# The last store inside each exit block, and the last head pair's q and k loaded one iteration sooner, in an attention and mixture-of-experts kernel

## The chip, the cores and the metric

The kernel runs on one core of a Trainium2 chip. The metric is the device time of one execution in microseconds (us), over several runs; lower is better. One further execution is profiled, and all rows below are from that one. A head pair is two of the 48 (batch, head) combinations whose q and k are handled together; SP is the engine (SyncE) whose queue issues nearly all plain DMAs here.

## The reference

Causal attention over 4 batches of 12 heads, 448 positions, head size 64, and then a mixture of experts in which each of the 1792 tokens goes to the one expert of eight with the highest gate value:

```python
scores = scale * np.matmul(q, k.transpose(0, 1, 3, 2))
scores = np.where(mask, -1000000000.0, scores)
attn = softmax(scores)                       # in the reference's words: max, exp, sum, divide
x = np.matmul(attn, v) -> (1792, 768)
logits = x @ w_gate + modality_bias[modality_id]
e_idx = np.argmax(logits, axis=1)
for e in range(8):
    h = np.maximum(x[e_idx == e] @ w1[e], 0.0)          # 768 -> 1024
    out[e_idx == e] = gate_w[e_idx == e, None] * (h @ w2[e])   # 1024 -> 768
```

(The lines are shortened.) All is float32. The kernel gets float32 accuracy from TensorE by splitting operands into a high and a low part in the type fp32r and adding up several products.

## The kernel before, in words

The order of the work is written out by hand: the function `iteration(n)` (from line 1150) issues for n from 0 to 47 one step of a software pipeline, and each engine takes its instructions in the order in which they are issued. In iteration n the scores of head n are computed (`st_scores`, line 279: matmuls L297 on TensorE (PE), mask and row maximum L306 on VectorE (DVE)), the exponentials of head n-1 (ScalarE (ACT), L316), the transposes of head n-2 (PE, L328, split into high and low by ACT, L345, and DVE, L346), the product with v of head n-3 (PE, L359 and L366), and the output of head n-4, which PE combines at L420. Lists of further pieces (`later`, `before`, `soon`) are run at named iterations by `run_todo`: among them the stores of the attention's result x to DRAM (SP, L463), the loads of the first expert's weights w1 (SP, L719), the splits of these on GpSimd (POOL, L727 and L728), the gathers of x rows for the first blocks (POOL, L784), and the schedule of the experts' blocks (DVE and POOL, lines 560 to 640).

The q and k of pair m come in these steps. `load_qk(m)` loads both, 448 KB, on SP. `split_qk(m)`, on POOL, makes the high parts and q's low part (L196, L197); `stack_qk(m)`, on SP, copies them inside SBUF with four DMAs (L215 and L216) into a tile of its own, of which there are three in turn (m modulo 3), two of them in the pool and one elsewhere; `split_kl(m)` makes the rest on POOL. The last pair, m = 23 (`LATE`, line 239), goes another way: `late_load` (lines 241 to 250) loads plain q and k without a split straight into the tile of pair 20, with three DMAs (k at L244, the two halves of q at L248) and two memsets on POOL (L247), and its scores use two matmul operands instead of four. Pair 20's last reader is the scores of head 41; the first reader of pair 23's tile is the scores of head 46, and the first reader of pair 22's is the scores of head 44. In the kernel before, `late_load(23)` is issued in iteration 42, behind `st_scores(42)` and that iteration's `run_todo`, and `stack_qk(22)` at the head of iteration 41, ahead of `st_out`, the to-do list and the scores.

Behind the attention come the expert steps: eight fixed ones (t = 0 to 7), and then up to 16 small steps t = 8 to 23 (`tail(t)`, line 1474), each inside the If of the one before it (`tc.If(total > t)`), where `total` is a number that the schedule computed on the chip. Here total is 10, so that the small steps 8 and 9 run, and at t = 10 all engines branch out of the nest. A small step handles one half block of 64 rows. It ends with its second products on PE (`small_g2`, matmuls L878 and L882); their scaling with the gate value and the indirect store to the output are done by `half_y` (line 1394: ACT L924, DVE L925 for the two halves of a row, then POOL's indirect DMA, L1398) at the head of the next step, with the table `idg[(t - 1) % 3][0]` of row numbers and gate values. As the step that is last is only known on the chip, each small step copies its table into one fixed tile, `glast` (two DVE copies, L1463 to L1465), and behind the whole nest `half_y(glast)` (L1481) does it once more for the step that was last. `glast` is filled with an out-of-range row number at the start (POOL memset, L986).

At the If's exit the engines bring their semaphores to the values that the blocks not run would have left; in the profile these instructions have the line of the If, L1475. Behind the kernel's last line all engines drain their queues and meet; these instructions have L1522.

Of the kernel before, what the change touches and what calls it, by code (L numbers as in the profile page):

```python
# [11 lines left out]
I32 = mybir.dt.int32  # L12
# [9 lines left out]
def attention_moe(  # L22
# [58 lines left out]
    def cst(name, shape, dt=F32):  # L81
        return const.tile(shape, dt, name=name)
# [41 lines left out]
    tri0 = ctri = cst("ctri", [128, E, E])  # L124
    modi = cst("modi", [128, B * NTL, 2], I32)
    bias_sb = cst("bias_sb", [128, NM, 1, E])
    glast = cst("glast", [128, 2], I32)

    w1h, w1l = [], []
    raw1 = [early.tile([128, DF], F32, name=f"raw1{k}") for k in range(K1)]  # L130
# [110 lines left out]
    def late_load(m):  # L241
        b, j = divmod(m, H // 2)
        t = st_tile(m, F32)
        nc.sync.dma_start(out=t[:, 0, 1], in_=qk[b, j, :, 1])  # L244
        for a in range(2):
            r = slice(a * 64, a * 64 + 64)
            P.memset(t[64 - a * 64:128 - a * 64, a, 0], 0.0)  # L247
            nc.sync.dma_start(out=t[r, a, 0], in_=qk[b, j, r, 0])  # L248
            spl[2 * m + a] = (t[:, a, 0], t[:, 0, 1], None, None)

    vraws = [vraw, raw1[2].rearrange("p (t c) -> p t c", t=NTL)]

# [26 lines left out]
    def st_scores(g):  # L279
        qs, ks, qh, kl = spl.pop(g)  # L280
        banks = [bank("sa"), bank("sb")]
        nm = sm([128, NTL], "nm")
        p = praw[g % 3]

        outs, parts = {}, []
        for i, last in SORD:
            q0, n = QT[i]
            w = q0 + n
            bk, c0 = SPOS[i]
            if not last:  # L290
                outs[i] = banks[bk][:n, c0:c0 + w]
            if last and qh is None:
                continue
            a, z = (qh, kl) if last else (qs, ks)
            r = 128 if qh is None else n
            z0 = (128, 64, 64, 0)[i]
            nc.tensor.matmul(  # L297
                banks[bk][:r, c0:c0 + w], lhsT=a[:, q0:q0 + r], rhs=z[:, z0:z0 + w],
                start=(last == 0), stop=(last == 1 or qh is None),
            )  # L300
        for i in ORD:
            n = QT[i][1]
            w = QT[i][0] + n
            parts.append((i, n, outs[i], masks[i][:n], p[:n, POFF[i]:POFF[i] + w]))
        for i, n, o, m, z in parts:
            V.tensor_tensor_reduce(  # L306
                out=z, in0=o, in1=m, scale=-scale, scalar=3.0e38, op0=ALU.add, op1=ALU.min,
                accum_out=nm[:n, i:i + 1],
            )
        sc[g] = (p, parts, nm)  # L310
# [618 lines left out]
    with tc.manual_schedule():  # L929
# [53 lines left out]
        cthi = it[:, 64:64 + E * MAXB].rearrange("p (e b) -> p e b", b=MAXB)  # L983
        ctri_i = it[:, 192:192 + E * E].rearrange("p (e f) -> p e f", f=E)
        ti = it[:, 256:257]
        P.memset(glast, BIG)  # L986
        P.memset(onesf, 1.0 / STEP)
        P.memset(eq, 0.5)
        P.memset(sch_a, -float(STEP * SHIFT + 1))
# [29 lines left out]
        def run_todo(n):  # L1019
            for f in todo.pop(n, ()):  # L1020
                f()
# [127 lines left out]

        def iteration(n):  # L1150
            split = 7 < n + 3 < NHEAD and n + 3 >> 1 not in LATE
            if n % 2 == 1 and split:
                stack_qk((n + 3) // 2)
            gr, i = divmod(n - 2 * GH, GH)
            comb = 0 <= gr < B * NG
            if 0 <= n - 4 < NHEAD:
                st_out(n - 4)
            if comb:
                st_move(gr, i)
                st_norm(gr, i)  # L1160
                b, u = divmod(gr, NG)
                if u == NG - 1:
                    later(n + 1, lambda i=i: x_store(b, i))
                    if i == NTL - 1:
                        after_batch(b, n)
            run_todo((n,))
            if n in (2, 3):
                st_trans(n - 2)
            if n < NHEAD:
                st_scores(n)  # L1170
            run_todo(n)
            if n == 0:
                split_vh(0)
            if n % 2 == 1 and split:
                split_kl((n + 3) // 2)
            if n % 2 == 0 and 7 < n + 4 < NHEAD:
                (late_load if n + 4 >> 1 in LATE else split_qk)((n + 4) // 2)
            if n % GH == 1 and n > GH:
                st_sums(n // GH - 1)
            if n % GH == RECAT and n > GH:  # L1180
                st_rec(n // GH - 1)
            if 0 <= n - 1 < NHEAD:
                st_exp(n - 1)
            if 0 <= n - 2 < NHEAD:
                if n > 3:
                    st_trans(n - 2)
                run_todo(-n)
                st_split(n - 2)
            if 0 <= n - 3 < NHEAD:
                st_pv(n - 3)  # L1190
                st_low(n - 3)
            gr, i = divmod(n - 2 * GH + 1, GH)
            if 0 <= gr < B * NG:
                st_comb(gr, i)
            if n == 1:
                split_vl(0, V)
            if n == 2 or n % GH == 3 and n > GH and n // GH + 1 < B * NG:
                split_vh(n // GH + 1)
            if n == 2 or n % GH == 0 and n > GH:
                split_vl((n + 2) // GH, P)  # L1200
            if n == 4:
                V.memset(vraws[1][0:64, 3, :], 0.0)
            if n in (1, 3, 5, 7):
                load_qk(4 + n // 2)
            if n % 2 == 0 and n > 7 and n + 8 < NHEAD and n + 8 >> 1 not in LATE:
                load_qk((n + 8) // 2)
            if n in (1, 4):
                load_v(n // GH + 1)
            if n == 1:
                clear_tables()  # L1210
            if n % GH == 2 and n > GH and n // GH + 2 < B * NG:
                load_v(n // GH + 2)
# [190 lines left out]
        def step(t):  # L1403
            if t > SZ:
                half_y(idg[(t - 1) % 3][0])
            if SZ - 1 <= t and t + 1 < NSTEP:
                tc.mark_branch_hint_location(f"tail{t + 1}", reg(sch[t:t + 1, 5:6], HINTED, 0, 1), HINTED)
            ids_for(t + 2)
            nw = is_new(t)
            if t == 1:  # L1410
                with tc.If(nw < 1):
                    prefetch(0, raw1, w1, K1)
                    prefetch(0, raw2, w2, K2)

            wa, wb = (range(K2), None) if t < PZ else (range(K2 // 2), range(K2 // 2, K2))

            def w2_a():
                with tc.If(nw > 0):  # L1418
                    split_w(raw2, w2h, w2l, wa)
                    if wb is None:  # L1420
                        prefetch(t, raw2, w2, K2)

            def w2_b():
                with tc.If(nw > 0):
                    split_w(raw2, w2h, w2l, wb)
                    prefetch(t, raw2, w2, K2)

            def mid():
                if t + 1 == NSTEP:
                    return  # L1430
                next_x(t + 1, [x for _ in places_of(t + 1) for x in two_banks()])
                if t + 2 < NSTEP:
                    fetch_x(t + 2)
                with tc.If(is_new(t + 1) > 0):  # L1434
                    new_w1(t + 1)

            u = t % 2
            if t < PZ:
                w2_a()
                g1_pair()  # L1440
                part2(t, 0, of_pair(0), lambda: None, mid, [bank("ot"), bank("x")])
                ys = ht_banks()
                g2(ys, of_pair(1), range(K2))
                y_out(t, 1, ys)
                return
            if t < SZ:
                hb, pb = part1(u, w2_a, w2_b)
                part2(t, 0, of_block(u), lambda: h_trans(u, hb, 1, pb), mid, [bank("ot"), bank("x")])
                return
            oa, ob = two_banks()  # L1450
            pa, pb = ht_banks()
            w2_a()
            for k in range(4):
                for half, o in enumerate((oa, ob)):
                    small_g1(u, half, o, [k])
            for half, o in enumerate((oa, ob)):
                small_g1(u, half, o, range(4, K1))
                small_h(half, o)
            small_trans(u, 0, pa)
            small_trans(u, 1, pb)  # L1460
            w2_b()
            mid()
            g = idg[t % 3][0]  # L1463
            V.tensor_copy(glast[:, 0:1], g[:, 0:1])
            V.tensor_copy(glast[:, 1:2].bitcast(F32), g[:, 1:2].bitcast(F32))  # L1465
            small_g2(yl, u, range(2))
            for n in range(2):
                small_g2(yl, u, range(2, K2), [n])
# [3 lines left out]
        yl = [bank("ot"), bank("x")]  # L1472

        def tail(t):
            with tc.If(total > t, label=f"tail{t}"):  # L1475
                step(t)
                if t + 1 < NSTEP:
                    tail(t + 1)

        tail(SZ)  # L1480
        half_y(glast)  # L1481


_INS = ['qk', 'v', 'moe_modality_id', 'moe_w_gate', 'moe_modality_bias', 'moe_w1', 'moe_w2']
# [42 lines left out]
```

## Time and profile before

| | us |
|---|---|
| median of 3 runs | 489.51 |
| lowest and highest | 488.55, 492.07 |
| profiled execution, its own time | 491.61 |
| span of the profile | 489.9 |

| engine | busy us | share of the span | instructions |
|---|---|---|---|
| PE, matmul | 470.4 | 96% | 3219 |
| PE, weight load | 433.7 | 89% | 3219 |
| DVE | 291.6 | 60% | 864 |
| ACT | 277.9 | 57% | 696 |
| POOL | 237.1 | 48% | 320 |

The span runs from the first to the last instruction of the profiled execution; what the device time has beyond it lies around it. In the rows below a timeline's line gives start, duration, engine, line of the kernel, operation, output and input by their names in the program, shapes, and a count where equal neighbours are put together; what stands in brackets is the idle time of that engine just before, and what the profile takes to have ended it. A q behind an engine's name is its instruction queue: issues of DMAs, semaphores and branches. PEclk, the granted clock, is in parts of the full one. An attention iteration takes some 3.5 us in the stretch around 160 us.

### The profile page before, as it was taken

How to read it: one execution, taken by the hardware profiler on the slowest of the kernel's cores; microseconds unless marked ns; L12 is line 12 of the kernel's file. 1: busy time of each engine (PE TensorE's matmuls, PEld its weight loads, DVE VectorE, ACT ScalarE, POOL GpSimd, SP SyncE). 2: the span in 40 equal slices, each digit the busy share in tenths (PEclk: the TensorE clock that was granted, in tenths of full speed). 3: DMA queues.
4: the chain of work that ended last, by engine and by line, in shares of the span. 5: the costliest groups of instructions: out<-in, count | busy, mean ns of one | idle time of the engine just before them, and what ended most of it. 6: DMA issues, size and time to landing. Idle time of an engine off the chain costs nothing.

```text
span 489.9 us, 10098 instructions
## 1 busy us (share of the span) xinstructions
PE 470.4 (96%) x3219; PEld 433.7 (89%) x3219; DVE 291.6 (60%) x864; ACT 277.9 (57%) x696; POOL 237.1 (48%) x320
## 2 busy tenths in 40 slices
PE   8999999999999989989999999999999999999991
PEld 6789998998899868879999999999999999889770
DVE  7999999999999968787211126620130110283591
ACT  6899999999999967253312125620221111483670
POOL 7997999999999969952202004102001001021131
PEclk9999999999999989999999999999999999999997
DMA  7799789998996595523693006833001001086200
GB/s 191 221 261 250 210 218 282 247 228 237 242 238 148 135 314 189 185 91 97 194 411 111 33 1 226 304 118 101 33 0 55 33 14 52 33 285 204 96 15 4
DMA packets 43303, 77.25 MB, mean 158 GB/s; under 512 B 15582, under 2 KB 27614, under 8 KB 43232
## 3 DMA queue, kind: packets, MB, share of 16 engines
q1 hardware_dynamic: 40112, 65.30, 46.4%
q0 software_dynamic: 3040, 11.03, 6.6%
q8 instruction: 27, 0.44, 0.4%
q14 instruction: 44, 0.36, 0.2%
q10 hardware_dynamic: 80, 0.11, 0.1%
HBM read 48.10 MB, written 12.08 MB: 123 GB/s over the span
## 4 chain that ended last, share of the span: by engine, by line
PE 65%; DVE 14%; ACT 7%; issue 5%; POOL 4%; DMA 3%; POOLq 0%; DVEq 0%; ACTq 0%
PE g L803 7%; PE g L804 7%; PE g L805 7%; PE pt L328 4%; PE sa L297 4%; PE sb L297 4%; DVE p L306 3%; DVE pl L346 3%; ACT p L316 3%; PE ot L359 3%; PE ot L366 3%; PE x L420 2%; ACT ph L345 2%; PE ot L804 2%; DVE ut L390 2%
## 5 line engine op out<-in xcount | busy, mean ns | idle before, releaser
L784 POOL DMA_INDIRECT xg<-xs,idg x18 | 21.1, 1172 | 157.3 <-DVEq L1434 81.1
L316 ACT ACTIVATE p<-p,nm 128x448 f32<-128x448 f32 x192 | 94.7, 497 | 2.2 <-POOL eq L1039 1.9
L822 DVE SCALAR_TENSOR_TENSOR htl<-g,hth 128x256 fp32r<-128x256 f32 x40 | 16.7, 424 | 106.1 <-ACT hth L821 106.1
L803 PE MATMUL g<-xh,w1h 128*128 128x256 f32 x240 | 67.9, 283 | 0.3 <-DVE htl L822 0.3
L804 PE MATMUL g<-xl,w1h 128*128 128x256 f32 x240 | 67.8, 283 | 0.0
L805 PE MATMUL g<-xh,w1l 128*128 128x256 f32 x240 | 67.4, 281 | 0.0
L346 DVE TENSOR_TENSOR pl<-pt,ph 128x1024 fp32r<-128x1024 f32 x48 | 58.2, 1215 | 6.3 <-ACT ph L345 5.7
L345 ACT ACTIVATE ph<-pt 128x1024 fp32r<-128x1024 f32 x48 | 49.1, 1022 | 6.7 <-PE pt L328 5.9
L359 PE MATMUL ot<-ph,vhl 128*128 128x448 f32 x192 | 50.2, 302 | 2.0 <-DVE ut L390 1.0
L821 ACT ACTIVATE hth<-g 128x256 fp32r<-128x256 f32 x40 | 15.1, 382 | 65.0 <-PE g L805 62.0
L328 PE MATMUL pt<-ident,p 128*128 128x128 f32 x384 | 50.4, 275 | 0.0
L328 PEld LDWEIGHTS pt<-ident,p 128*128 128x128 f32 x384 | 45.5, 142 | 2.4 <-issue 0.7
L805 PEld LDWEIGHTS g<-xh,w1l 128*128 128x128 f32 x240 | 45.6, 190 | 0.0
L863 POOL DMA_INDIRECT out_dram<-row,idg x14 | 16.7, 1192 | 59.5 <-ACTq L1418 29.3
L803 PEld LDWEIGHTS g<-xh,w1h 128*128 128x128 f32 x240 | 45.0, 187 | 0.5 <-DVE htl L822 0.5
L804 PEld LDWEIGHTS g<-xl,w1h 128*128 128x128 f32 x240 | 45.0, 188 | 0.0
L306 DVE CUSTOM_DVE_ANT_0 p<-sa,mask 128x448 f32<-128x448 f32 x96 | 36.1, 412 | 3.4 <-PE sa L297 1.7
L359 PEld LDWEIGHTS ot<-ph,vhl 128*128 128x128 f32 x192 | 32.8, 189 | 5.8 <-DVE ut L390 1.8
L306 DVE CUSTOM_DVE_ANT_0 p<-sb,mask 128x192 f32<-128x192 f32 x96 | 36.3, 412 | 0.4 <-PE sb L297 0.4
L316 ACT ACTIVATION_READ_ACCUMULATOR p<-p,nm 128x1 f32 x192 | 36.4, 189 | 0.0
L366 PE MATMUL ot<-pl,vhl 128*64 128x64 f32 x192 | 34.5, 294 | 0.5 <-DVE pl L346 0.4
L390 DVE TENSOR_TENSOR ut<-ot,hol 64x448 f32<-64x448 f32 x48 | 29.4, 612 | 1.5 <-ACT hol L384 0.8
(389 smaller groups left out, 1298.2 us busy)
## 6 DMA issues: line engine op xcount, KB each, us to landing
raw<-in_moe_w_dram SPq DMA_DIRECT2D x24, 512.0 KB
st<-hl SPq DMA_DIRECT2D x52, 224.0 KB
raw<-in_qk_dram SPq DMA_DIRECT2D x19, 448.0 KB
raw<-in_moe_w_dram SPq DMA_DIRECT2D x20, 384.0 KB
vraw<-in_v_dram SPq DMA_DIRECT2D x7, 384.0 KB
w1h<-hl SPq DMA_DIRECT2D x12, 224.0 KB
w1l<-hl SPq DMA_DIRECT2D x12, 224.0 KB
xs<-row SPq DMA_DIRECT2D x6, 384.0 KB
```

Of the source, the lines that this page charges most:

```text
L297: nc.tensor.matmul(banks[bk][:r, c0:c0 + w], lhsT=a[:, q0:q0 + r], rhs=z[:, z0:z0 + w], start=(last == 0), stop=(last == 1 or qh is None),)
L306: V.tensor_tensor_reduce(out=z, in0=o, in1=m, scale=-scale, scalar=3.0e38, op0=ALU.add, op1=ALU.min, accum_out=nm[:n, i:i + 1],)
L316: A.activation(out=z, in_=z, func=AF.Exp, bias=nm[:n, i:i + 1], scale=-1.0, accum_out=sums[:n, b, i, h:h + 1],)
L328: nc.tensor.transpose(out=o, in_=a, identity=ident)
L345: A.activation(out=ph, in_=t, func=AF.Copy)
L346: V.tensor_tensor(out=pl, in0=t, in1=ph.bitcast(F32), op=ALU.subtract)
L359: nc.tensor.matmul(o[:, q0:q0 + c1 - c0], lhsT=t[:, n, h].rearrange("p a d -> p (a d)"), rhs=ph[:, c0:c1], start=(n == 0), stop=(n == 1),)
L366: nc.tensor.matmul(o[0:D, q0:q0 + c1 - c0], lhsT=t[:, n, h, 0], rhs=pl[:, c0:c1], start=False, stop=False)
L390: V.tensor_tensor(out=ots(gr, j)[a * 64:a * 64 + 64], in0=ov.pop(g)[0:64, :S], in1=ol.pop(g), op=ALU.add)
L803: nc.tensor.matmul(o, lhsT=ah, rhs=bh, start=first, stop=False)
L804: nc.tensor.matmul(o, lhsT=ah, rhs=bl, start=False, stop=False)
L805: nc.tensor.matmul(o, lhsT=al, rhs=bh, start=False, stop=last)
```

## The change

There are two edits.

First, the tile `glast`, its memset and the two copies per small step are removed. The last `half_y` is no longer behind the nest but in the nest's exits: each If of the small steps from t = 9 on gets an Else block that does `half_y` with the table of step t - 1 directly, and the innermost block, of step 23, does it behind its own step. Only one of these 16 places runs in an execution; here that is the Else block of t = 10.

Second, `late_load(23)` is issued in iteration 41, behind `st_scores(41)` and ahead of that iteration's to-do list, directly in front of `stack_qk(22)`, which for this one pair moves from the head of iteration 41 to the same place. The two memsets stay in iteration 42, as `late_zeros`.

```diff
-    glast = cst("glast", [128, 2], I32)
...
         for a in range(2):
             r = slice(a * 64, a * 64 + 64)
-            P.memset(t[64 - a * 64:128 - a * 64, a, 0], 0.0)
             nc.sync.dma_start(out=t[r, a, 0], in_=qk[b, j, r, 0])
             spl[2 * m + a] = (t[:, a, 0], t[:, 0, 1], None, None)
+
+    def late_zeros(m):
+        for a in range(2):
+            P.memset(spl[2 * m + a][0][64 - a * 64:128 - a * 64], 0.0)
...
-        P.memset(glast, BIG)
...
             split = 7 < n + 3 < NHEAD and n + 3 >> 1 not in LATE
-            if n % 2 == 1 and split:
+            ahead = n + 5 >> 1 in LATE
+            if n % 2 == 1 and split and not ahead:
                 stack_qk((n + 3) // 2)
...
             if n < NHEAD:
                 st_scores(n)
+            if n % 2 == 1 and ahead:
+                late_load((n + 5) // 2)
+                stack_qk((n + 3) // 2)
             run_todo(n)
...
             if n % 2 == 0 and 7 < n + 4 < NHEAD:
-                (late_load if n + 4 >> 1 in LATE else split_qk)((n + 4) // 2)
+                (late_zeros if n + 4 >> 1 in LATE else split_qk)((n + 4) // 2)
...
-            g = idg[t % 3][0]
-            V.tensor_copy(glast[:, 0:1], g[:, 0:1])
-            V.tensor_copy(glast[:, 1:2].bitcast(F32), g[:, 1:2].bitcast(F32))
...
         def tail(t):
-            with tc.If(total > t, label=f"tail{t}"):
+            with tc.If(total > t, label=f"tail{t}") as there:
                 step(t)
                 if t + 1 < NSTEP:
                     tail(t + 1)
+                else:
+                    half_y(idg[t % 3][0])
+            if t > SZ:
+                with there.Else():
+                    half_y(idg[(t - 1) % 3][0])
 
         tail(SZ)
-        half_y(glast)
```

## Rows read from the trace of the kernel before

**Rows 1.** Windows; columns: busy us per engine, granted clock, DMA share, GB/s.

```profile
157.00:161.30 4.30, 4.30 (x35) 4.03 (x34) 4.27 (x16) 4.25 (x14) 4.30 (x6) 1.00 0.45 142
174.10:176.30 2.20, 0.05 (x2) 0.06 (x1) 2.20 (x7) 2.17 (x9) 2.07 (x4) 1.00 1.08 178
177.10:180.50 3.40, 3.40 (x14) 2.90 (x13) 1.55 (x8) 0.00 (x0) 2.32 (x1) 0.50 0.88 322
184.10:225.10 41.00, 39.24 (x236) 33.11 (x234) 34.66 (x103) 20.47 (x44) 29.73 (x32) 1.00 0.43 135
225.10:479.00 253.90, 253.16 (x1682) 241.67 (x1682) 84.09 (x176) 86.42 (x156) 39.40 (x31) 1.00 0.34 117
```

**Rows 2.** Timeline of PE, 156 to 177 us; [idle before <-releaser] last.

```profile
155.99 0.31 PE L297 MATMUL sb<-xh,qz 128*128 128x320 f32 x1
...
166.77 0.47 PE L297 MATMUL sa<-st 128*128 128x448 f32 x1
...
173.47 0.65 PE L420 MATMUL x<-wi,ut 128*128 128x144 f32 x4
176.27 1.02 PE L297 MATMUL sa<-st 128*128 128x448 f32 x2 [2.15 <-DVE ltp L439]
```

**Rows 3.** Timeline of SP, 157 to 177 us.

```profile
157.74 0.36 SPq L719 DMA_DIRECT2D raw<-in_moe_w_dram  x1
161.35 0.49 SPq L215 DMA_DIRECT2D st<-hl  x1
...
170.00 0.38 SPq L244 DMA_DIRECT2D st<-in_qk_dram  x1
170.44 1.32 SPq L248 DMA_DIRECT2D st<-in_qk_dram  x2
...
175.98 0.33 SPq L463 DMA_DIRECT2D xs<-row  x1
```

**Rows 4.** Waits of SP's queue, 140 to 200: us, times, longest.

```profile
SPq L463 <- DMA st<-in_qk_dram: 0.6, 1, 0.6
```

**Rows 5.** Timelines of ACT, POOL and DVE, 177 to 212 us.

```profile
180.93 1.02 ACT L345 ACTIVATE ph<-pt 128x1024 fp32r<-128x1024 f32 x1 [4.66 <-PE pt L328]
...
177.07 2.35 POOL L728 TENSOR_TENSOR w1l<-raw,w1h 128x1024 fp32r<-128x1024 f32 x1
...
183.03 0.24 POOL L439 TENSOR_TENSOR ltp<-cxt,rec 128x32 f32<-128x32 f32 x1 [3.61 <-ACT cxt L430]
...
184.33 1.10 POOL L784 DMA_INDIRECT xg<-xs,idg  x1 [0.49 <-DVE idg L783]
...
211.82 0.60 DVE L630 TENSOR_TENSOR mask<-ctri,q 128x64 f32<-128x64 f32 x3 [0.30 <-POOL ctri L616]
```

**Rows 6.** Timeline of the end, 478 to 490 us.

```profile
478.71 0.28 PE L878 MATMUL x<-w2h,hth 128*128 128x256 f32 x1
479.17 0.68 ACT L924 ACTIVATE hol<-ot,glast 64x512 f32<-64x512 f32 x1 [3.34 <-PEq L1475]
...
482.53 0.74 DVE L925 SCALAR_TENSOR_TENSOR row<-ot,glast,hol 64x512 f32<-64x512 f32 x1 [4.72 <-DMA out_dram<-row,idg]
483.20 0.47 DVE L925 SCALAR_TENSOR_TENSOR row<-x,glast,ltp 64x256 f32<-64x256 f32 x1
483.94 0.93 POOL L1398 DMA_INDIRECT out_dram<-row,glast  x1 [4.80 <-DVE row L925]
```

**Rows 7.** Line 1475 (the tail's If): duration ns, first and last start us.

```profile
L1475 POOLq INC_SWDGE_SEM  x1: 1183/1183/1183, 481.3 to 481.3; - x1
```

**Rows 8.** Line 1522 (behind the kernel): duration ns min/median/max, first and last start us.

```profile
L1522 SPq EVENT_SEMAPHORE  x13: 17/28/28, 482.4 to 489.8; - x13
...
L1522 POOLq DRAIN  x3: 40/118/5338, 483.7 to 489.6; - x3
```

**Rows 9.** Waits of SP's queue, 464 to 490: us, times, longest.

```profile
SPq L1522 <- DMA out_dram<-row,glast: 3.4, 1, 3.4
```

**Rows 10.** Line 863 (the 14 stores of whole blocks), POOL.

```profile
DMA to landing us min/median/max: 3.1/4.2/5.3
```

## The prediction

> **What bounds the kernel now.** I read the table of windows first, then the timelines of the engines at the two places that the diff touches, then the waits of SP's queue, and last the kernel's end. From 225.1 to 479.0 us PE is busy 253.16 of 253.90 us, and from 184.1 to 225.1 it is busy 39.24 of 41.00 [rows 1]. So PE is the bound behind the attention loop, and whatever PE is late by at 184 us is carried to the last matmul. Two places are not like that. At 174.1 to 176.3 PE does 0.05 us of work in 2.20, while the DMA share is 1.08; and from 177.1 to 180.5 PE is busy all 3.40 us, but at a granted clock of 0.50, the lower of its two levels (1.2 GHz instead of 2.4) [rows 1]. The other is behind the last matmul.
>
> The first hole is the place of part b. The scores of head 46, the first of pair 23, start at 176.27 after 2.15 us of idleness; the combination before them ended at 173.47 + 0.65 = 174.12 [rows 2]. The row names a DVE operation (ltp, L439) as releaser. I do not believe it: SP issues pair 23's three loads only at 170.00 to 171.76, and SP's next x store, at 175.98, has itself waited 0.6 us for the load "st<-in_qk_dram" [rows 3, 4]. So that load was under way until about 175.9, and its reader starts 0.3 us later. The load takes about 5.9 us from its first issue, in a stretch in which the DMA engines are full.
>
> The second place is the end. The last matmul ends at 478.71 + 0.28 = 478.99. ACT scales from 479.17 on, but DVE's first instruction starts at 482.53, ends with its second at 483.67, and POOL's store runs from 483.94 to 484.87 [rows 6]. What DVE waited for has no instruction of the computation in it: at the If's exit POOL has one instruction that adjusts a DMA semaphore, from 481.3, for 1.183 us [rows 7], so to 482.48, 0.05 us ahead of DVE. Then POOL's DRAIN runs from 483.7 for 5.338 us, to 489.04, which is 489.04 - 484.87 = 4.17 behind the end of the store's instruction [rows 6, 8].
>
> **The change part by part.** All sums are made against the profiled execution, 491.61 us (span 489.9 and 1.7 around it); the median of the runs shown is 489.51, which is 2.10 less, and I carry the difference over.
>
> *Part b, the earlier loads.* Three DMAs move by one iteration, with no instruction added. SP's weight load of 157.74 takes it to 158.1, and its next copy, pair 22's first, starts at 161.35 [rows 3]. The new place is between these, and the tile's former readers (head 41's scores) end at 155.99 + 0.31 = 156.30 [rows 2], so the issue needs no wait. It costs SP 0.38 + 1.32 = 1.70 us [rows 3], so to about 159.8, within the 3.25 us that SP stands idle there. With the 5.9 us that the loads take now, they land at 158.1 + 5.9 = 164.0, some 10 us ahead of 174.12. The DMA share at 157.0 to 161.3 is 0.45 [rows 1], so they should rather land sooner.
>
> What is queued behind them on SP is pair 22's four stack copies. These start when SP has them, at 161.35 as now, and their first reader is at 166.77 [rows 2]. If the new 448 KB were still under way in front of them, at the 322 GB/s that the full stretch moved [rows 1] they would hold the copies 1.4 us at most; the copies have 5.4 us until their reader. I take 0 for that; the bound is +1.4. The memsets stay in their iteration, 0.
>
> What goes is PE's wait of 2.15 us [rows 2]. What follows it goes too, if the clock fell because PE had stood still: 3.40 us of work at half clock would be 1.70 at full, so up to 1.70 more. That is PE's bound, 3.85. The next thing late would be POOL: its weight split ends at 177.07 + 2.35 = 179.42, and from there POOL stands idle 3.61 us until 183.03; ACT's hole, until 180.93, is 4.66 [rows 5]. Behind it POOL issues the gather of 184.33, works on, and at 211.82 DVE's schedule waits for POOL [rows 5], so a gain that POOL does not make isn't kept there. POOL's weight split does not move, so about 3.6 is what it can give, near PE's 3.85. I take **-3.7**, with bounds 0 (the wait is another) and -4.7 (ACT's whole hole). SP is free 1.7 us sooner at 170, which lets the x store go sooner; worth 0, since nothing read here waits for it.
>
> *Part a, the exit arms.* The four small copies to glast (two in each of the two small steps of this run) go from DVE, which is busy 84.09 of 253.90 us there, beside a PE that is idle 0.74 us in all that time [rows 1]: 0, bound -0.74. One memset of two columns on POOL goes: 0, bound the 0.24 of POOL's short row [rows 5].
>
> In the new arm the scaling no longer stands behind the If's exit, so DVE need not wait for POOL's adjustment. ACT's first result is there at 479.17 + 0.68 = 479.85, DVE needs 1.14 us and ends at 481.0 with 0.05 for the start, the store follows 0.27 later as now: 481.3 to 482.3, which is 2.6 us sooner [rows 6]. But the arm must still even out its semaphores for the blocks not run, and it has one DMA more under way than the If's exit had: this store. SP's wait for it is 3.4 us from 482.4 [rows 8, 9], so it lands at about 485.9, 1.9 to 2.0 after its issue. In the changed kernel that is 481.3 + 2.0 = 483.3. If the adjustment then comes behind the store and takes 1.18 [rows 7], POOL is free at 484.5; with 0.2 for the branch and the same 4.17 behind it, the DRAIN ends at 488.85, against 489.04. So I take **-0.2**: the 2.6 us won in front are paid back by an adjustment that moves from before the store to behind it. Bounds: -2.6, if all behind the store keeps its distance to it; +1.0, if the DRAIN takes its 5.34 from when it is reached, 484.7 + 5.34 = 490.04.
>
> A rule of the Trainium skill speaks against this part. By "DMA: Bandwidth & Descriptors", section "Anatomy of one DMA — SWDGE (gpsimd) path", one such transfer takes about 2.0 us and on top of it its bytes at 436 GB/s. For 64 rows of 3072 bytes that would be an estimate of 2.45 us, where the rows show 1.9 to 2.0 [rows 6, 9]. By the page's figure the store would land 0.5 later and part a be +0.3, the whole 485.9 instead of 485.6; I go by the row.
>
> Sum: 491.61 - 3.7 - 0.2 = 487.7 for a profiled execution, and 489.51 - 3.9 = **485.6** for the median.
>
> **Rivals.**
> 1. *The arm gives its full 2.6.* The adjustment stands ahead of the arm's body on an idle POOL, or needn't wait for the store. For it: the DRAIN was reached at 483.7, before the store's instruction began [rows 6, 8], so its end may hang on the store alone. Against it: the one adjustment in the trace stands where the paths meet, and waited until 481.3 [rows 7]. Then -3.7 - 2.6 = -6.3: 483.2.
> 2. *Head 46 doesn't wait for its load, or another wait takes its place.* For it: the row names DVE's ltp [rows 2], and DVE is busy 2.20 of 2.20 us in the hole, ACT 2.17, POOL 2.07 [rows 1], which is how a loop looks that is bound there anyway. Against it: SP's wait on that very load ends beside it [rows 4]. Then part b gives nothing to a third, and the sum is -0.2 to -1.4; I take -0.8: 488.7.
> 3. *Slower: a serial chain in POOL's queue at the end.* The arm's adjustment waits for the store's landing, and only then comes the DRAIN, from its start. The other indirect stores of this kernel land in 3.1 to 5.3 us [rows 10]. With 5.3: 481.3 + 5.3 + 1.2 + 0.1 + 5.34 = 493.3, against 489.04: +4.3, with part b +0.6: 490.1. It decides from where the chain behind the store's issue is over (489.04 - 481.3) + 3.7 = 11.4 us. Against it: this store landed within 2.0, with only 64 rows and nothing beside it.
> 4. *The change does not do what it says* (the scheduler holds the earlier load behind some other wait, or the arm's code is late to arrive): -0.2 to +1, with the rest.
>
> **How the numbers follow.** The forecast 0.53, with its own range from 484.3 (clock and ACT's bound in full, a little of the tail) to 487.0 (no clock gain, tail +0.2); rival 1 0.18; rival 2 0.17; rival 3 0.07; rival 4 and the rest 0.05. The range reaches from below rival 1, less half a microsecond for the spread of runs, 482.8, to above rival 2, 489.2, which leaves out rival 3, the rest, and some edges of the others. One per cent is 4.9 us, which is about what a measurement of this kernel can tell from no change: below 484.6 counts as faster. That holds for rival 1 nearly whole, and for the low edge of the forecast and of the rest, some 0.10 more: 0.27. Above 494.4 needs rival 3 with a bad run or something unseen: 0.04. The rest, 0.69, is within.
>
> **What would show it.** For part b: pair 23's three loads issued at about 158 to 160, no idle time ahead of head 46's scores at about 174.1, a granted clock of 1.00 from 175 to 178 us, POOL's hole gone at 179, and the last matmul at about 475.3 instead of 479.0. A hole of 2 us that stays with another releaser is rival 2. For part a: DVE's last scaling within 0.2 us of ACT's first result, the store about 1.3 us after that, POOL's adjustment behind the store's landing, and as much time as before (10.0 us) from the last matmul to the DRAIN's end; 7.5 there is rival 1, over 14 rival 3. What would make the prediction wrong altogether is a new wait of pair 22's scores at 166 to 167 us for its stack copies.

## The result, and the profile after

The changed kernel takes 483.36 us (median of 4 runs, 482.88 to 483.62), the kernel before beside it 490.19 (4 runs, 488.55 to 492.07): ratio 0.9852, 95% interval 0.9825 to 0.988. Run again later, it took 483.24 (5 runs, 483.12 to 483.59) against 490.86 (15 runs): 7.6 us, 0.9854 (0.9819 to 0.9888). The forecast was 485.6, with 482.8 to 489.2 as its range; the time fell on rival 1's 483.2, though, as the runs show, only partly for rival 1's reasons. The span went from 489.9 to 481.4. Times below are medians, and differences in us are between medians; the ratios are estimated over all runs of a pair, so the two need not agree to the last digit, as the kernel before spreads over 4 us. Two runs among the experiments, of 2588.14 and 1625.22 us, stand outside all figures below; what held them is not known.

What answers to [rows 1], about the same stretches of the work, some microseconds earlier:

```profile
156.30:160.60 4.30, 4.30 (x36) 4.07 (x34) 4.30 (x15) 4.23 (x15) 4.24 (x5) 1.00 0.65 191
173.30:175.60 2.30, 2.30 (x15) 1.72 (x14) 2.30 (x7) 2.21 (x9) 2.11 (x4) 1.00 0.81 222
176.40:179.80 3.40, 3.40 (x24) 2.80 (x23) 3.34 (x13) 3.35 (x10) 3.25 (x4) 1.00 0.98 383
180.20:218.40 38.20, 36.47 (x219) 30.80 (x219) 32.05 (x95) 17.93 (x38) 29.21 (x32) 1.00 0.48 155
218.40:471.00 252.60, 251.50 (x1680) 240.03 (x1680) 85.16 (x173) 88.16 (x159) 37.80 (x30) 1.00 0.35 117
```

The hole is gone from the second line (PE busy 2.30 of 2.30) and the half clock from the third (1.00 instead of 0.50). The extra 448 KB show in the first: 0.65 instead of 0.45 of the DMA engines. The fifth line holds a surprise: it covers nearly as much work as before's 253.90 us (1680 matmuls for 1682) in 252.60, with the clock at 1.00 in both.

PE's timeline answers to [rows 2], SP's to [rows 3]:

```profile
155.24 0.31 PE L299 MATMUL sb<-xh,qz 128*128 128x320 f32 x1
...
172.72 0.65 PE L422 MATMUL x<-wi,ut 128*128 128x144 f32 x4
173.21 0.92 PE L299 MATMUL sa<-st 128*128 128x448 f32 x2
...
175.05 1.04 PE L330 MATMUL pt<-ident,p 128*128 128x128 f32 x8
```

```profile
156.97 0.36 SPq L721 DMA_DIRECT2D raw<-in_moe_w_dram  x1
157.43 0.38 SPq L243 DMA_DIRECT2D st<-in_qk_dram  x1
157.87 1.15 SPq L246 DMA_DIRECT2D st<-in_qk_dram  x2
160.57 0.48 SPq L214 DMA_DIRECT2D st<-hl  x1
```

The loads sit in SP's gap, as worked out; pair 22's copies start 0.78 us sooner than before, as all does there, and not later. Head 46's scores follow the combination without idle time. In the kernel before, the eight transposes behind these scores are this row, to be held against the 1.04 us above:

```profile
179.22 1.68 PE L328 MATMUL pt<-ident,p 128*128 128x128 f32 x8
```

And the end, which answers to [rows 6 to 9]: the timeline, the If's line, the line behind the kernel, and SP's waits. The second and third fence hold the last gather of x rows, in the kernel before (L784) and in the changed one (L786): it is the last transfer that POOL starts ahead of the exit.

```profile
471.54 0.68 ACT L926 ACTIVATE hol<-ot,idg 64x512 f32<-64x512 f32 x1 [1.88 <-PE ot L880]
...
472.33 0.74 DVE L927 SCALAR_TENSOR_TENSOR row<-ot,idg,hol 64x512 f32<-64x512 f32 x1 [1.04 <-ACT hol L926]
472.55 0.28 PE L880 MATMUL x<-w2h,hth 128*128 128x256 f32 x1
472.92 0.47 ACT L926 ACTIVATE ltp<-x,idg 64x256 f32<-64x256 f32 x1 [0.70 <-PEq L1477]
473.42 0.47 DVE L927 SCALAR_TENSOR_TENSOR row<-x,idg,ltp 64x256 f32<-64x256 f32 x1 [0.35 <-ACT ltp L926]
474.68 0.93 POOL L1403 DMA_INDIRECT out_dram<-row,idg  x1 [1.70 <-POOLq L1477]
```

```profile
478.17 0.97 POOL L784 DMA_INDIRECT xg<-xs,idg  x1 [5.24 <-DVE glast L1465]
```

```profile
472.00 0.97 POOL L786 DMA_INDIRECT xg<-xs,idg  x1 [4.63 <-PE ot L880]
```

```profile
L1477 POOLq INC_SWDGE_SEM  x1: 1184/1184/1184, 475.0 to 475.0; - x1
```

```profile
L1528 POOLq DRAIN  x3: 40/113/4159, 476.4 to 481.1; - x3
...
L1528 POOLq INC_SWDGE_SEM  x1: 765/765/765, 473.1 to 473.1; - x1
```

```profile
SPq L1528 <- DMA out_dram<-row,idg: 0.5, 1, 0.5
```

ACT's and DVE's first part of the scaling now begins before the last matmul is over; in the kernel before, ACT waited for the branch out of the nest. The store starts 1.85 us after the last matmul's end (472.83), where it took 4.95. POOL's adjustment of 1.18 us stands behind the store, and does not wait for it: it starts at 475.0, 0.3 after the store began. A second, shorter one (0.77 us from 473.1, the last line of the fifth fence), which the kernel before does not have, stands in front of the store in POOL's queue. The store starts 0.79 us behind DVE's end (473.89), where it took 0.27 in the kernel before, so in the arm POOL's queue holds it and not DVE. Nothing is lost by that: the store's instruction is over at 475.61, before the DRAIN starts. From the last matmul to the DRAIN's end it is 476.4 + 4.16 - 472.83 = 7.7 us, before 10.05.

The lead of this profile over that of before, place by place: 0.75 us at 155 us, ahead of any change (155.99 to 155.24); 3.06 at head 46's first score (176.27 to 173.21), so the hole gave 2.31; 4.81 behind the transposes (180.90 to 176.09), so the clock gave 1.75; 6.16 at the last matmul, so 1.35 more came in the expert stretch; 8.5 at the DRAIN's end, so the tail gave 2.36. The 0.75 arises in the kernel's first 7 us, in which of this change only the memset of glast acts (0.10 us on POOL), and went down to 0.3 in the second profile of the same kernel. In the six profiles of kernels that keep glast the same score starts at 155.05 to 155.99: it is scatter of the start, and no part of the effect.

### The profile page after: what moved, and what is told of

It reads as the page before. It is cut to its first block, busy times and chain, and to the rows that moved or that the text cites. A ratio compares the mean times of both kernels' runs of the same rounds, so it can differ in the third digit from the quotient of the medians.

```text
span 481.4 us, 10091 instructions
## 1 busy us (share of the span) xinstructions
PE 466.1 (97%) x3219; PEld 430.2 (89%) x3219; DVE 291.1 (60%) x860; ACT 278.0 (58%) x696; POOL 236.3 (49%) x319
## 5 line engine op out<-in xcount | busy, mean ns | idle before, releaser
L786 POOL DMA_INDIRECT xg<-xs,idg x18 | 21.0, 1169 | 156.5 <-DVEq L1439 81.1
L805 PE MATMUL g<-xh,w1h 128*128 128x256 f32 x240 | 67.1, 279 | 0.4 <-DVE htl L824 0.4
L805 PEld LDWEIGHTS g<-xh,w1h 128*128 128x128 f32 x240 | 44.9, 187 | 0.6 <-DVE htl L824 0.6
```

The lines of the kernel that those rows point to most:

```text
L786: P.indirect_dma_start(out=xg[u][:n], out_offset=None, in_=xs[0:rows, :], in_offset=bass.IndirectOffsetOnAxis(ap=g[:n, 0:1], axis=0), boun ...
L805: nc.tensor.matmul(o, lhsT=ah, rhs=bh, start=first, stop=False)
```

## The experiments

**1. Each part alone.** The first run has the diff's second edit only, the second run its first edit only.

> Part b alone: glast, its copies and the last store behind the nest stay as before. Theory (the hole and the slow clock behind it are the load's, and are worth all that part b gave): head 46's scores start without a gap, the granted clock stays at 1.00 behind it, and PE is 2.3 + 1.7 = 4.0 us earlier at 180 us than in the kernel before; the MoE stretch is no faster than before (mean of the first-product matmuls 283 ns, as tiles lie where they lay), and the end from the last matmul to the DRAIN's end is 10.0 us as before. Total about 4.0 below before: ratio 0.992. Rival (the arms or the removed tile gave part of the 4.0): less than 3, ratio 0.994 or above. Rival (the MoE stretch is faster because the transfers behind 176 us come sooner): another 1.3 us, ratio 0.989, with first-product matmuls at 279 ns.

Measured: 487.20 us (6 runs, 487.05 to 487.79) against 491.29 (20 runs, 488.78 to 493.02), ratio 0.9929 (0.9903 to 0.9955): 4.1 us, as expected. No idle time ahead of head 46, the clock at 1.00 behind it; first-product matmuls (L803 to L805 in the kernel before, `g`) 281 to 283 ns by line, as before; tail (from the last matmul to the DRAIN's end) 10.0 us.

> Part a alone: glast, its memset and copies gone, the last store in the exit arms; the late load stays in iteration 42. Theory: the 2.15 us hole at 174 us and the half clock behind it stay; the end is 7.7 us instead of 10.0, worth 2.4; and as the removed tile lets xh, xl and the other tiles behind it move 32 bytes down, the first-product matmuls take 279 ns instead of 283, worth 1.3 over the MoE stretch. Total -3.7: ratio 0.9925. Rival (the faster matmuls are not due to part a): -2.4, ratio 0.995, matmuls at 283 ns. Rival (the tail's gain needs the earlier load): the end still takes 10 us, ratio 0.997 or above.

Measured: 488.19 (9 runs, 485.57 to 489.46), ratio 0.9935 (0.9909 to 0.9961): 3.1 us, where the theory had 3.7; this kernel and the one before both keep the late load and spread over some 4 us. Tail 7.7 us; hole and clock loss still there; and the matmuls of `g` took 279 to 280 ns. So the faster expert stretch belongs to part a, no edit of which touches these matmuls.

**2. Where the tiles lie.** Part a removes a tile. The constants lie one behind the other in SBUF, each in a multiple of 32 bytes, and what comes behind glast, `xh` and `xl` (the experts' inputs, read by every `g` matmul) among it, lies 32 bytes lower; the first expert weights stay where they were. The third run puts an unused tile in its place, the fourth adds one to the kernel before:

```diff
     bias_sb = cst("bias_sb", [128, NM, 1, E])
+    cst("space", [128, 2], I32)
```

> The changed kernel with an unused tile of 8 bytes in glast's place, so that the tiles behind it lie where they lay in the kernel before; no instruction differs. Theory (the place of the tiles sets the rate of the first-product matmuls): 283 ns instead of 279, PE 1.3 us later at the end of the MoE stretch, 1.3 us slower than the changed kernel: about 484.7, ratio 0.988 to before. Rival (the 1.3 us differ from run to run, or come from the copies to glast that are gone): the same as the changed kernel, 279 ns, ratio 0.985.

Measured: 484.71 (6 runs, 484.43 to 485.34), ratio 0.9875 (0.9849 to 0.9901), against the changed kernel's 483.24 to 483.36: 1.4 us slower without a different instruction. `g` is back at 281 to 283 ns, the tail stays at 7.6 us. So the place of the tiles is shown to be the cause. It also isolates the arms: this kernel differs from the load-alone run by part a's instructions only, 487.20 - 484.71 = 2.5 us.

> The kernel before with one more unused tile of 8 bytes behind glast, so that the tiles behind it lie 32 bytes higher; no instruction differs. Theory (what counts is whether xh and xl lie at an even or odd multiple of 32 bytes): first-product matmuls at 279 ns instead of 283, 1.3 us faster than before, ratio 0.9973. Rival (the place does not matter): same as before, ratio 1.000, 283 ns.

Measured: 490.54 (11 runs, 487.89 to 492.73), ratio 0.9991 (0.9965 to 1.0018), `g` at 284 to 285 ns. The rule of even and odd multiples of 32 fell; this place is as slow as the kernel before's. Three more places, with 96, 128 and 160 bytes instead of 8 in the same line of the changed kernel:

> The changed kernel with an unused tile of 96 bytes in glast's place, so that the tiles behind it lie 96 bytes higher than in the changed kernel, 64 above those of the kernel before; no instruction differs. So far one first-product matmul follows the other by 120.2 ns (place of the kernel before), 117.9 ns (32 bytes below) and 120.0 ns (32 above). Theory (it goes by the place of xh and xl, relative to the weights', in steps of 32 bytes, with a period of 128): a fourth value, anywhere from 117 to 121 ns; the time follows it by 0.6 us for each ns. Rival (a period of 64 bytes, with an odd outlier): as the place of the kernel before, 120.2, and about 484.7 us.

> The changed kernel with an unused tile of 128 bytes in glast's place, so that the tiles behind it lie 128 bytes higher than in the changed kernel; no instruction differs. Theory (a period of 128 bytes in the place of xh and xl): 117.7 to 117.9 ns from one first-product matmul to the next, as in the changed kernel, and its time, 483.4. Rival (lower places are better, or the four values found so far have no period): another spacing, 118.5 to 120.2, and 0.5 to 1.4 us more.

> The changed kernel with an unused tile of 160 bytes in glast's place: the tiles behind it lie 160 bytes higher than in the changed kernel, one step of 32 above the fastest place so far; no instruction differs. From one first-product matmul to the next it took 117.7 ns at the changed kernel's place, then 120.0, 119.8, 118.7 and 113.5 at 32, 64, 96 and 128 bytes above. Theory (the spacing falls further for some steps, with a longer period than 128 bytes): 113.5 ns or less, 480.5 us or less. Rival (one good place among bad ones): 117 to 120 ns, 483 to 484.7 us. No working from rows says which; the two have about equal chances.

| xh and xl, bytes above the changed kernel's | from one `g` matmul to the next, ns | median us |
|---|---|---|
| 0 (the changed kernel) | 117.7 | 483.24 |
| 32 (third run; the kernel before lies here too) | 120.0 | 484.71 |
| 64 (fourth run, a kernel before) | 119.8 | 490.54 (11 runs) |
| 96 | 118.7 | 483.92 (2 runs) |
| 128 | 113.5 | 480.45 (3 runs, 479.91 to 481.0) |
| 160 | 118.3 | 483.56 (5 runs) |

A period of 128 bytes, and a spacing that goes on falling, both fell: it is one good place among six, and what makes it good is open. The spacing is the mean from start to start in PE's timeline, between `g` matmuls that follow one another without a gap, and it goes by the place alone: six profiles of kernels whose tiles lie as in the kernel before, with the late load or without, with the exit arms or without, all give 120.0, and four with the changed kernel's place all give 117.7. These rows are the same two matmuls of three kernels (before, the changed one, and that with 128 bytes), 96 matmuls apart:

```profile
242.35 0.28 PE L803 MATMUL g<-xh,w1h 128*128 128x256 f32 x1
...
253.87 0.28 PE L803 MATMUL g<-xh,w1h 128*128 128x256 f32 x1
```

```profile
237.57 0.28 PE L805 MATMUL g<-xh,w1h 128*128 128x256 f32 x1
...
248.87 0.28 PE L805 MATMUL g<-xh,w1h 128*128 128x256 f32 x1
```

```profile
237.49 0.28 PE L806 MATMUL g<-xh,w1h 128*128 128x256 f32 x1
...
248.37 0.28 PE L806 MATMUL g<-xh,w1h 128*128 128x256 f32 x1
```

11.52, 11.30 and 10.88 us for 96 matmuls; the duration column shows 0.28 in all. There are 720 of them, so 2.3 ns each are 1.65 us, where the runs give 1.5, and 4.2 ns are 3.0, where they give 2.8 (480.45 against 483.24). **The 128-byte kernel, 0.9796 of before (0.9755 to 0.9837), is faster than both kernels:** its slowest run (481.0) lies below the changed kernel's fastest (482.88). It has three runs only, and whether it is 2% below before is unclear, as the interval lies on both sides of that.

**3. The wait and the clock.** To part the two, 36 products of a constant tile fill the hole of the kernel before:

```diff
+        if g == 46:
+            for _ in range(36):
+                nc.tensor.matmul(banks[0][:, 0:128], lhsT=ones, rhs=ones, start=True, stop=True)
         for i, last in SORD:
```

> The kernel before, with 36 extra products of a constant tile (128 columns each) put into the scores' bank in front of head 46's scores; their result is overwritten by these. They fill PE's hole, while the load still comes late. Theory (two costs in one: the wait of about 2 us, and a clock that falls because PE stood still): the wait stays, but the granted clock behind it stays at 1.00, and from the first of head 46's scores to the last of the transposes behind them it takes 2.5 us as in the changed kernel instead of 4.2: 1.2 to 1.7 below before in such a profile, ratio 0.997. Rival (the clock falls for another reason, such as the load of the DMA engines or what came ahead): still 4.2 us, ratio 1.000. Rival (the wait is not the load's but DVE's): the extra products run at once and push the scores, ratio 1.002 or more.

Measured: 489.57 (12 runs, 488.9 to 491.72) against 490.88 (23 runs), 1.3 us less, ratio 0.9979 (0.9959 to 0.9998). PE's timeline, and the window behind it:

```profile
173.08 2.17 PE L288 MATMUL sa<-ones 128*128 128x128 bf16 x36
175.24 0.99 PE L300 MATMUL sa<-st 128*128 128x448 f32 x2
...
177.16 1.04 PE L331 MATMUL pt<-ident,p 128*128 128x128 f32 x8
```

```profile
177.00:180.50 3.50, 3.50 (x26) 2.96 (x25) 2.44 (x9) 2.22 (x4) 1.73 (x2) 1.00 0.98 380
```

The load is about as late as before (the scores start some 6 us behind its first issue in both) and the DMA engines as full (0.98), but the clock stays at 1.00: from the first score to the last transposes' end it is 177.16 + 1.04 - 175.24 = 2.96 us, in the kernel before 180.90 - 176.27 = 4.63. So the 1.67 us of the clock come from PE's own standing still.

The profiles of the kernels that keep the late load show how its landing varies. Arms alone, the extra tile behind glast, and the run of point 5 in turn:

```profile
175.28 1.69 PE L296 MATMUL sa<-st 128*128 128x448 f32 x2 [2.11 <-DVE ltp L438]
```

```profile
174.72 0.99 PE L298 MATMUL sa<-st 128*128 128x448 f32 x2 [1.53 <-DVE pl L347]
```

```profile
174.93 0.99 PE L297 MATMUL sa<-st 128*128 128x448 f32 x2 [1.32 <-DMA st<-in_qk_dram]
```

One wait, three names. The DVE names change from run to run, and the third row names the load. The trace's records of landings settle it: in the kernel before, with arms alone, with the extra tile and with the hole filled, the first of head 46's scores starts 0.14 us behind the last landing on record of its half of q (176.13 and 176.27 in the kernel before). Over 176 to 181 us the granted clock was 0.66 in the kernel before, behind its 2.15 us of standing still, and 0.72 with arms alone, behind 2.11; in the other two, behind 1.53 and 1.32, it was 1.00. So the load costs from some 1.3 us to 4 an execution, and that goes with the spread: 488.78 to 493.02 in before's 20 runs, at most 1.1 us in the runs of each kernel that loads at iteration 41. That the load makes all of the spread isn't shown: the second kernel of point 4 spreads over 5 us, though its profile has no gap at head 46.

**4. In front of the copies, or only earlier.** Two kernels: the two calls of the change swapped, and then the late load of the kernel before moved only to the head of iteration 42. The first:

```diff
             if n % 2 == 1 and ahead:
+                stack_qk((n + 3) // 2)
                 late_load((n + 5) // 2)
-                stack_qk((n + 3) // 2)
```

> The changed kernel with the last pair's loads behind pair 22's four stack copies instead of in front of them; all else the same. Theory (any place that has the load landed by 173 us gives the same): SP issues it at about 163.8 to 165.5, it lands by about 169 to 171, head 46's scores start without a gap: the same time as the changed kernel, about 483.4. Rival (the place in front of the copies is what counts): the loads now queue behind copies, stores and table reads, land after 173, and 1 to 3 us come back: 484.5 to 486.5.

Measured: 485.16 (4 runs, 485.05 to 485.98): 1.8 to 1.9 us of the gain lost. The time is in the rival's range, but neither theory had the place. There is no gap at head 46 (173.35), the load is in time; but the later DMAs of SP's queue come some 2 us later, and so does this, on POOL and then on PE:

```profile
180.51 0.61 POOL L451 TENSOR_TENSOR row<-cxt,rec 128x256 f32<-128x256 f32 x1 [1.48 <-DMA xs<-row]
181.28 1.10 POOL L786 DMA_INDIRECT xg<-xs,idg  x1 [0.16 <-DMA raw<-in_moe_w_dram]
```

```profile
213.92 0.69 PE L807 MATMUL ot<-w2h,htl 128*128 128x384 f32 x1 [2.27 <-DVE htl L836]
```

```profile
213.00:218.00 5.00, 4.08 (x15) 4.08 (x16) 4.69 (x18) 1.48 (x3) 0.97 (x1) 0.66 0.03 1
```

POOL waits for a row tile whose x store SP issued late; the gather is 1.64 us later than the changed kernel's (179.64), and at 214 PE waits 2.27 instead of 0.59 and falls to a clock of 0.66. PE's lag behind the changed kernel grows from 0.14 us at head 46 to 1.87 at the last matmul. The links between this gather and the wait at 214 are not shown here row by row. So SP's gap ahead of the copies is worth 1.8 us: there the loads push nothing.

The second kernel, against the kernel before:

```diff
         def iteration(n):
             split = 7 < n + 3 < NHEAD and n + 3 >> 1 not in LATE
+            if n % 2 == 0 and n + 4 >> 1 in LATE:
+                late_load((n + 4) // 2)
             if n % 2 == 1 and split:
                 stack_qk((n + 3) // 2)
...
-                (late_load if n + 4 >> 1 in LATE else split_qk)((n + 4) // 2)
+                (late_zeros if n + 4 >> 1 in LATE else split_qk)((n + 4) // 2)
```

> The kernel before with the late load alone moved, but only to the head of its own iteration 42: in SP's queue in front of the first four table reads and of a weight load and an x store, behind pair 22's copies and the x store ahead of it. Tail and tiles as before. Theory (SP's gap ahead of pair 22's copies is what makes the move free; anywhere behind it the loads push SP's table reads by some 1.7 us, the gathers and the schedule behind them come later, and PE waits for these at about 214 us): no gap in front of head 46's scores, but some 1 to 2 us of PE's gain are given back behind 210 us, with a lower clock there: 1.0 to 2.0 above the load-alone run's 487.2, so 488.2 to 489.2. Rival (what counts is only that the load lands by 173): 487.2.

Measured: 488.90 (10 runs, 487.12 to 492.2), ratio 0.9972 (0.9947 to 0.9996): 1.7 above the load-alone run, in the theory's range. But the execution that was profiled (487.52) shows no gap at head 46 and only the 0.59 us at 213, so what the others wait for was not seen: for this kernel the mechanism stays open.

**5. What holds the last store.** The kernel before, with its last scaling written into an idle staging tile, which is none of the four row tiles:

```diff
-        def half_y(g):
-            y = row()
+        def half_y(g, y=None):
+            y = row() if y is None else y
...
-        half_y(glast)
+        half_y(glast, raw1[0][:, 0:DM])
```

> The kernel before with its last scaling written into another tile (the staging tile of w1's first part) instead of one of the four row tiles, so that DVE need not wait for the semaphore of the row tiles' stores. Theory (DVE is held by that one semaphore, which POOL brings up only behind the gather's landing, and POOL itself is held by the same): DVE scales right behind ACT, about 2.6 us sooner, but POOL's store still comes behind its adjustment, at about 482.8 on before's scale instead of 483.9; the end from the last matmul to the DRAIN's end is 8.8 to 9.0 us instead of 10.0, ratio 0.998. Rival (leaving the nest holds DVE itself): DVE and the end as before, 10.0 us. Rival (POOL is not held, only DVE): 7.5 us.

Measured: 491.16 (10 runs) against 490.88, ratio 1.0004 (0.9978 to 1.003).

```profile
476.20 0.68 ACT L924 ACTIVATE hol<-ot,glast 64x512 f32<-64x512 f32 x1 [3.35 <-PEq L1475]
476.79 0.46 ACT L924 ACTIVATE ltp<-x,glast 64x256 f32<-64x256 f32 x1
476.92 0.74 DVE L925 SCALAR_TENSOR_TENSOR raw<-ot,glast,hol 64x512 f32<-64x512 f32 x1 [2.10 <-ACT hol L924]
477.59 0.47 DVE L925 SCALAR_TENSOR_TENSOR raw<-x,glast,ltp 64x256 f32<-64x256 f32 x1
480.75 0.93 POOL L1398 DMA_INDIRECT out_dram<-raw,glast  x1 [4.59 <-issue]
```

```profile
L1475 POOLq INC_SWDGE_SEM  x1: 1183/1183/1183, 478.2 to 478.2; - x1
```

DVE is free, 2.6 us sooner against the last matmul, and nothing to speak of comes of it: tail 9.8 us, where the other kernels with this tail have 9.9 to 10.1. The store starts 1.35 us behind the end of POOL's adjustment (479.4), as it had started 1.48 behind it in the kernel before. So DVE's wait held the store by 0.13 us at most; what held it was POOL's queue, in which it stands behind the adjustment. My theory put the store at 0.3 behind the adjustment, and fell by that microsecond.

**6. The changed kernel again.**

> The changed kernel itself, beside the same runs of the kernel before. Theory: 483.4, in a narrow spread of under 1 us, as there is no late load left whose landing varies; the difference from before is the sum of the parts measured singly, 4.1 (load) + 2.3 (exit arms) + 1.4 (place of the tiles) = 7.8, so 0.984. Rival (parts overlap or hinder each other): a difference outside 7.0 to 8.6.

Measured: 483.24, spread 0.47, 7.6 below before, as expected. The sum 4.1 + 2.5 + 1.5 = 8.1 is no test of whether the parts add up: it goes step by step from the kernel before (491.29) over the load alone (487.20) and the extra tile (484.71) to the changed kernel (483.24), and differs from 7.6 only by the two medians of before. The test is part a alone with part b alone: 3.1 + 4.1 = 7.2 against 7.6, which agrees within the spread of the kernels with the late load.

## Why the prediction was right, and where it was not

*What bounds the kernel:* right. PE's lead at 180 us reached the last matmul.

*Part b, -3.7:* right, a little small, by the mechanism that it states: 4.1 by the load-alone run, 2.31 + 1.75 in the profile. Of my bounds PE's 3.85 was the nearer; POOL did not hold it back. The step that took the x store's earlier issue as worth nothing was wrong in its reason: in the swapped run POOL waits 1.48 us for just such a store. In the changed kernel SP is early enough that this chain keeps up with the faster PE; 2 us later it does not. Rival 2 was wrong: the profile's name for the wait (DVE ltp) was that of the last event, not of the cause. Rival 4 did not come about: SP issued the loads where the edit put them.

*Part a, -0.2:* wrong by ten times, and this is the step that failed: "the arm must still even out its semaphores ..., and it has one DMA more under way", from which I had the adjustment wait until the store had landed. The adjustment does stand behind the store, but it starts 0.3 us after the store began, at 475.0, while the store lands only at about 476.7, where SP's wait of 0.5 us for it ends. What it follows in each profile is the last gather: 3.1 us behind its issue in the kernel before (481.3), 3.0 in the changed one and in the run of point 5. By the trace's records of landings this gather's last one comes at 481.25 in the kernel before and at 474.96 in the changed one, and in every one of the fourteen profiles the adjustment starts 0.02 to 0.03 us behind it. It waits for what was under way before the arm, not for the arm's own store; what an earlier gather would give was not tried. So POOL was free at 476.2, where my steps, moved by PE's 6.16 us, have it at 478.3, and the DRAIN followed with its 4.16, as assumed. The tail gave 2.36 in the profile, 2.5 in the runs: rival 1's term of 2.6, by the second of its two conditions (the adjustment "needn't wait for the store"). Rival 3 asked for a chain of over 11.4 us behind the store's issue; it was 5.9.

The store's transfer, 1.9 to 2.0 us by the rows, took 2.0 to 2.1 in the changed kernel. By the Trainium skill ("DMA: Bandwidth & Descriptors", section "Anatomy of one DMA — SWDGE (gpsimd) path") it would be 2.45 us as an estimate; the trace does not bear that out. It decided nothing: SP waited 0.5 us for the landing, but POOL's adjustment and DRAIN, which end last, did not. The whole that the prediction names for the page's figure is added up wrongly: 489.51 - 3.7 + 0.3 is 486.1, and not 485.9. In rival 3 the chain ends at 493.24, so that it is 4.2 behind before and not 4.3.

*What no step had:* the tile's removal. I cost glast at its copies and memset, which are worth nothing; its 32 bytes are worth 1.5 us.

*The base:* 489.51 was the median of three runs of a kernel that spreads over 4 us; 20 later runs gave 491.29. That is why 483.2, worked out as -6.3, met a change of -7.6: the forecast's number and rival 1's both lacked the tiles' 1.5, and for rival 1 the low base made up for it, which is luck. The forecast's own range, 484.3 to 487.0, was missed; the wide one held, 0.6 from its lower end, because it was drawn to take in rival 1. And the time is below 484.6, the line from which the prediction counted a run as faster, to which it gave 0.27 against 0.69 for no such change.

## What to carry to other kernels

A transfer that is late by 2 us can cost 4, as it did here where PE behind it worked at the lower clock for 3.4 us; look at the granted clock behind each hole, and put the issue into a stretch in which its queue stands idle anyway, since a place some DMAs later gave 1.8 of the 4.1 us back. At the exit from this kernel's nest of blocks, what stands in the arm's own code went ahead of the adjustment that waits for the gather in POOL's queue, and what stands behind the nest went behind it. And after an edit that adds or removes any tile, compare the spacing of the matmuls with a control that keeps the other tiles in place; the place itself is worth trying in steps of 32 bytes.

## What was not expected of the hardware

The spacing of the `g` matmuls, 128 by 128 by 256 columns, went from 113.5 to 120.0 ns with the place of `xh` and `xl`, and of all else behind the removed tile, in steps of 32 bytes, at a granted clock of 1.00, in a pattern that six places don't settle. The busy share doesn't show it, as PE is busy throughout at each of these rates; the starts do. Whether it is the place of `xh`, of `xl`, or theirs against the weights' was not tried. The Trainium skill ("TensorE: Matmul & The Clock Gate", section "Step-by-step: what each phase is for") says that loading the next weights takes no read bandwidth from the running matmul, as each has a port of its own. If that holds here, the two don't contend for reads in these streams, and the cause lies elsewhere; no run here tells. What the runs show is that the place matters, and not by which way.
